# Retention and a gated feed-forward on one core: query order, the x^T blocks kept in DRAM, the work lists and the last products changed together

## The chip, the cores and the metric

The kernel runs on one core of one Trainium2 chip. The metric is the device time of one execution in microseconds (us). A second figure is the span of a profiled execution, from the first to the last instruction of the program that the profiler recorded; it is a little shorter than that execution's own time.

## The reference

For 8 batches and 8 heads, with 576 positions of 64 features, a masked retention is computed, and its result goes through a feed-forward layer:

```
scores = q @ k^T / 8                     # [8, 8, 576, 576]
ret    = scores * gamma_h ** (i - j)     # for i >= j, else 0
x      = (ret @ v), heads side by side   # [4608, 512]
h      = x @ w_in                        # [4608, 2048]
g      = h * erf(softplus(h))
out    = g @ w_out                       # [4608, 512]
```

Everything is float32. The decay lets `ret @ v` be computed in pieces of 128 positions, with a state (a sum of k^T v, 64 x 64 for each head) carried from piece to piece.

## The kernel before

**Attention.** 36 pieces of 128 token rows. Four pieces cover most of a batch (576 = 4 x 128 + 64) and the last 64 rows of two batches share a piece. One piece goes through three stages. `transposes(i)` brings q and k into the layout with features on partitions: for the first 8 pieces by TensorE and an eviction by ScalarE (L317), for the later ones by 32 x 32 transposes on VectorE (L310) of data that was loaded in squares. `scores(i)` computes k^T q by heads (L326) and masks it on VectorE into `sT`. `outputs(i)` multiplies by v (L342), adds the carried state times q (L353), computes the new state k^T v (L367), adds it to the old one in `sums` on VectorE, multiplies it by a decay (L384, GpSimd), asks for the loads of a later piece, scales v of the next piece on GpSimd (`weigh_values`, L298), and evicts to `x`. The list `stages` fixes the order of these stages, and `attend` takes them from it.

**Feed-forward.** Four pieces make a chunk of 512 tokens, `x[g, c]` with c from 0 to 8; the 2048 hidden features are worked in 4 groups g. A block (g, c) has a `First` (x times w_in) and a `Second` (times w_out), each in Strassen form: 7 products in place of 8, of 8 TensorE instructions each (L453, L559). `First` and `Second` of neighbouring blocks alternate, and pieces of attention stand between their products as long as there are any. The very first block uses the plain 8 products (`plain`, L507). Strassen's operands are sums of quarters: of x^T in `operands_x` (VectorE), of the activations in `sums` (VectorE), of the weights in `sums_in` and `sums_out`. `softplus` and `erf` run on ScalarE, each after a table load.

The products of a `Second` add up in PSUM: in tile `a` the products B11, T2, T1, B22 follow each other without clearing, and `take` reads `a` after each of them, into another quarter of `o`. So each of them waits for the take before it. `add` takes in the other products (tiles `e` and `g`).

**Kept in DRAM.** For g = 0 `store_x` writes a chunk of x^T with its Strassen sums to `xd`: 7 blocks of 512 columns (only 4 for c = 0); for g = 1 to 3 `load_x` reads it back. The partial sums of the output go to `od` and come back for the next group.

**Weights.** `load_weights` loads a raw piece, and `rounding` works it into the form used, step by step: two steps on ScalarE, four on VectorE, then a multiplication and an addition on GpSimd (L259, L260), after which the next piece is loaded. `round_weights(n)` takes n steps.

**Order.** Nothing is scheduled by a planner. Each engine executes its instructions in the order in which the program names them. A string of letters written by hand sets the start: `a` is one stage of attention, `p` one plain product, `w` two weight loads, `s` the store of chunk 0, a digit that many rounding steps. All loads and stores but one are issued from SyncE's queue, in program order; a queued transfer whose buffer isn't free holds up those behind it. The table of decays (`cst`) comes in over ScalarE's queue.

Of the kernel before, what the change touches and what calls it, by code (L numbers as in the profile page):

```python
# [11 lines left out]
FP32 = mybir.dt.float32  # L12
# [6 lines left out]
P = 128  # L19
# [3 lines left out]
CONST_COLS = H + NP * P + NP + P + H  # L23
# [7 lines left out]
def decays():  # L31

    gamma = 1.0 - 2.0 ** (-5.0 - np.arange(H, dtype=np.float64))
    pairs = gamma.reshape(2, NP)
    t = np.arange(P)
    gk = pairs.T.reshape(1, H) ** -t[:, None]
    row = pairs.repeat(D, axis=0)
    out = np.where(np.arange(NP) % 2 == 0, row, np.roll(row, D, axis=0))  # L40
    gq = out[:, :, None] ** t[None, None, :] / math.sqrt(D)
    gp = row**P
    tri = t[None, :] >= t[:, None]
    gk2 = gk[t % D]
    return np.concatenate([x.reshape(P, -1) for x in (gk, gq, gp, tri, gk2)], axis=1).astype(np.float32)
# [3 lines left out]
def kernel(  # L49
# [39 lines left out]
    xd = [dram.tile([P, n_dc + 3, TCH], FP32, tag="xd", name="xd") for _ in range(n_ch)]  # L89
# [18 lines left out]
    live = {}  # L108

# [45 lines left out]
    nc.scalar.dma_start(out=cst, in_=consts)  # L155
    ends = [0]
    for m in (H, NP * P, NP, P, H):
        ends.append(ends[-1] + m)
    gk, gq, gp, tri, gk2 = (cst[:, a:b] for a, b in zip(ends, ends[1:]))
    gq = gq.rearrange("p (a i) -> p a i", a=NP)  # L160
    gp = gp.unsqueeze(2).to_broadcast([P, NP, D])
    load(1)
    load(2, "kv")
# [62 lines left out]
    def rounding():  # L226


        while True:
# [29 lines left out]
            nc.gpsimd.tensor_tensor(out=r_f, in0=high_f, in1=r_f, op=ALU.mult)  # L259
            nc.gpsimd.tensor_tensor(out=a_f, in0=a_f, in1=r_f, op=ALU.add)  # L260
            load_weights()
# [12 lines left out]

    tri2 = cpool.tile([P, P], FP32, name="tri2")
    nc.vector.tensor_copy(out=tri2, in_=tri)
    nc.vector.memset(tri2[:D, D:], 0.0)

# [21 lines left out]
    def transposes(i):  # L300
        t = live[i] = loaded.pop(i)
        if i < SQUARES:
            weigh_values(i + 1)
        for name in "qk":
            tT = t[name + "T"] = att.tile([P, NP, P], FP32, tag=name + "T", name=name + "T")
            if i >= SQUARES:
                for _, _, n, r0 in pieces[i]:
                    a = r0 // SQ * D
                    squares = t[name + "s"][:, :, a : a + n // SQ * D].rearrange("p h (a d) -> p h a d", d=D)
                    nc.vector.transpose(  # L310
                        out=tT[:, :, r0 : r0 + n].rearrange("p h (r a) -> p h a r", r=SQ), in_=squares[:, :, :, :SQ]
                    )
            else:
# [3 lines left out]
                nc.scalar.copy(out=tT, in_=pt)  # L317
# [15 lines left out]
    def outputs(i):  # L333
# [5 lines left out]
        o = [ps_at.tile([P, 4, P], FP32, tag="at", name=f"o{j}") for j in range(2)]  # L339
        for p in range(NP):  # L340
            for e in range(2):
                nc.tensor.matmul(  # L342
                    o[p % 2][heads[(e + p) % 2], p // 2, :],
                    lhsT=t["v"][:, 2 * p + e, :],
                    rhs=t["sT"][:, e, p, :],
                    start=(p < 2),
                    stop=(not seen and p >= NP - 2),
                    skip_group_check=True,
                )
        for state, r0, n in seen:  # L350
            for p in range(NP):
                for e in range(2):
                    nc.tensor.matmul(  # L353
                        o[p % 2][heads[(e + p) % 2], p // 2, r0 : r0 + n],
                        lhsT=state[heads[e], p, :],
                        rhs=t["qT"][heads[e], p, r0 : r0 + n],
                        start=False,
                        stop=(p >= NP - 2),
                        skip_group_check=True,
                    )  # L360
        b, s0, n, _ = segments[0]
        if n == P:

            kv = o[0].rearrange("p a i -> p (a i)")[:, 2 * P :].rearrange("p (a d) -> p a d", a=NP)
# [66 lines left out]
    def operands_x(g, c):  # L431
# [8 lines left out]
        if g == 0:  # L440
            store_x(c)
# [302 lines left out]
```

## Time and profile before

| what | value |
|---|---|
| median of 3 runs | 1050.09 us (1050.07 to 1050.46) |
| profiled execution | 1053.23 us, span 1051.5 us |
| TensorE (PE) busy | 1025.0 us, 97% of the span |
| VectorE (DVE) busy | 640.9 us, 61% |
| ScalarE (ACT) busy | 378.3 us, 36% |
| GpSimd (POOL) busy | 132.7 us, 13% |
| moved by DMA | 192.23 MB, 183 GB/s over the span |
| mean granted clock of TensorE | 0.988 |

The time falls into five stretches: the start up to about 75 us, with the first pieces of attention and the plain block; a stretch to about 335 us in which attention stands between the products of the blocks with g = 0; the last three blocks with g = 0; the blocks with g = 1 to 3, which are products alone; and the end, from about 1025 us, where no `First` is left to stand between the products of the last `Second`s. In a timeline line the columns are start, duration, engine, line, operation, output<-inputs, shapes, and the count; in brackets stands how long the engine was idle ahead of it and what ended that.

### The profile page before, as it was taken

The numbers are of one execution on the slowest core, as the hardware profiler recorded it, in microseconds if no ns is written. First come the engines' busy times: TensorE is split into PE (matmuls) and PEld (weight loads), VectorE is DVE, ScalarE is ACT, GpSimd is POOL, SyncE is SP. The second block draws the span as 40 slices with busy tenths as digits, with TensorE's granted clock in tenths as the row PEclk, the third lists the DMA queues.
The fourth block names the chain that finished last, engine by engine and source line by source line (L and its number), as shares of the span: only waits on it lengthen the run. The fifth ranks groups of instructions, "written<-read, shape, count | busy, mean of one in ns | idle before, by whom it ended". The sixth has DMA issues, their size and how long they took to land.

```text
span 1051.5 us, 15730 instructions
## 1 busy us (share of the span) xinstructions
PE 1025.0 (97%) x6322; PEld 879.9 (84%) x6322; DVE 640.9 (61%) x1001; ACT 378.3 (36%) x459; POOL 132.7 (13%) x130
## 2 busy tenths in 40 slices
PE   8889999999899999999999999999999999999997
PEld 7667887778788888888888888888888888888885
DVE  3679888878677654555555655555556544454444
ACT  2243232231332444443434333434443333333341
POOL 2551321221221100100001000110100000000000
PEclk9889999999899999999999999999999999999999
DMA  9989979989995534544455455554343344454432
GB/s 195 254 169 237 242 193 256 217 226 244 219 256 167 188 112 150 190 170 170 159 195 197 155 192 205 189 191 151 150 150 121 150 169 176 165 202 167 171 121 80
DMA packets 146777, 192.23 MB, mean 183 GB/s; under 512 B 96016, under 2 KB 121104, under 8 KB 138640
## 3 DMA queue, kind: packets, MB, share of 16 engines
q1 hardware_dynamic: 146560, 190.88, 60.9%
q8 instruction: 50, 0.82, 0.3%
q10 hardware_dynamic: 144, 0.34, 0.1%
q14 instruction: 23, 0.19, 0.1%
HBM read 137.70 MB, written 53.48 MB: 182 GB/s over the span
## 4 chain that ended last, share of the span: by engine, by line
PE 80%; DMA 9%; DVE 5%; SPq 3%; issue 1%; POOL 0%; ACT 0%; DVEq 0%; POOLq 0%; ACTq 0%
PE a L559 22%; PE a L453 20%; PE g L559 11%; PE g L453 10%; PE e L559 5%; PE e L453 5%; DMA raw_ks<-in_k_dram 3%; SPq L137 2%; PE s L326 2%; DMA od<-o 2%; PE o L342 2%; DMA xd<-x 2%; DVE t L93 1%; DVE o L93 1%; PE o L367 1%
## 5 line engine op out<-in xcount | busy, mean ns | idle before, releaser
L453 PE MATMUL a<-x,wa 128*128 128x256 f32 x1120 | 266.0, 380 | 0.0
L453 PEld LDWEIGHTS a<-x,wa 128*128 128x128 f32 x1120 | 211.6, 190 | 29.4
L559 PE MATMUL a<-wb,s 128*128 128x256 f32 x864 | 205.8, 381 | 2.1 <-DVE o L93 2.1
L559 PEld LDWEIGHTS a<-wb,s 128*128 128x128 f32 x864 | 163.1, 190 | 26.2 <-DVE o L93 2.4
L93 DVE TENSOR_TENSOR o<-a,o 128x512 f32<-128x512 f32 x108 | 74.3, 688 | 107.0 <-PE a L559 104.2
L93 DVE TENSOR_TENSOR t<-g,t 128x512 f32<-128x512 f32 x70 | 48.3, 690 | 148.9 <-ACT t L483 112.5
L453 PE MATMUL g<-x,wa 128*128 128x256 f32 x560 | 133.4, 381 | 0.4 <-DVE o L93 0.3
L453 PEld LDWEIGHTS g<-x,wa 128*128 128x128 f32 x560 | 105.5, 190 | 16.4 <-DVE o L93 1.6
L259 POOL TENSOR_TENSOR wraw<-wraw 128x512 f32<-128x512 f32 x32 | 33.4, 1045 | 462.6 <-DVE wraw L258 242.6
L478 ACT COPY t<-a 128x512 f32<-128x512 f32 x35 | 20.5, 586 | 187.6 <-PE a L453 187.6
L93 DVE TENSOR_TENSOR t<-t,s 128x1024 f32<-128x1024 f32 x72 | 87.2, 1252 | 0.0
L522 ACT ACTIVATE s<-t 128x1024 f32<-128x1024 f32 x72 | 72.1, 1048 | 37.7 <-DVE t L93 37.6
L489 ACT COPY t<-a 128x512 f32<-128x512 f32 x35 | 20.5, 586 | 149.7 <-PE a L453 149.7
L559 PE MATMUL g<-wb,s 128*128 128x256 f32 x288 | 70.3, 388 | 3.8 <-DVE t L93 3.8
L526 ACT ACTIVATE s<-s 128x1024 f32<-128x1024 f32 x72 | 72.1, 1049 | 0.4
L559 PE MATMUL e<-wb,t 128*128 128x256 f32 x288 | 68.6, 381 | 0.0
L559 PE MATMUL a<-wb,t 128*128 128x256 f32 x288 | 68.6, 381 | 0.0
L559 PE MATMUL g<-wb,t 128*128 128x256 f32 x288 | 68.2, 380 | 0.0
L453 PE MATMUL e<-x,wa 128*128 128x256 f32 x280 | 66.7, 381 | 0.0
L559 PEld LDWEIGHTS g<-wb,s 128*128 128x128 f32 x288 | 55.4, 194 | 11.9 <-DVE t L93 4.1
L559 PEld LDWEIGHTS g<-wb,t 128*128 128x128 f32 x288 | 54.6, 190 | 7.5
L559 PEld LDWEIGHTS e<-wb,t 128*128 128x128 f32 x288 | 54.3, 190 | 7.7
(77 smaller groups left out, 1178.5 us busy)
## 6 DMA issues: line engine op xcount, KB each, us to landing
x<-xd SPq DMA_DIRECT2D x24, 1792.0 KB, 10.6
od<-o SPq DMA_DIRECT2D x54, 512.0 KB, 4.1
o<-od SPq DMA_DIRECT2D x27, 1024.0 KB, 7.0
xd<-x SPq DMA_DIRECT2D x8, 1792.0 KB, 7.2
raw_qs<-in_q_dram SPq DMA_DIRECT2D x96, 112.0 KB, 5.0
raw_ks<-in_k_dram SPq DMA_DIRECT2D x96, 112.0 KB, 4.4
raw_k<-in_k_dram SPq DMA_DIRECT2D x64, 128.0 KB, 4.5
raw_v<-in_v_dram SPq DMA_DIRECT2D x64, 128.0 KB, 4.7
```

Source lines behind the costliest of these rows:

```text
L93: nc.vector.tensor_tensor(out=out, in0=in0, in1=in1, op=op)
L137: nc.sync.dma_start(out=t[r0 : r0 + n, e::2, :], in_=heads.rearrange("h p d -> p h d"))
L259: nc.gpsimd.tensor_tensor(out=r_f, in0=high_f, in1=r_f, op=ALU.mult)
L326: nc.tensor.matmul(ps[e][:, p, :], lhsT=t["kT"][heads[e], p, :], rhs=t["qT"][heads[e], p, :], start=True, stop=True)
L342: nc.tensor.matmul(o[p % 2][heads[(e + p) % 2], p // 2, :], lhsT=t["v"][:, 2 * p + e, :], rhs=t["sT"][:, e, p, :], start=(p < 2), stop=(no ...
L367: nc.tensor.matmul(kv[heads[e], p, :], lhsT=t["k"][:, 2 * p + e, :], rhs=t["v"][:, 2 * p + e, :], start=False, stop=(p == NP - 1), skip_gr ...
L453: nc.tensor.matmul(acc[:, j * TH : (j + 1) * TH], lhsT=weights["wa", self.g][:, a, d, j * P : (j + 1) * P], rhs=x[self.g, self.c][a][:, d, :],
L478: nc.scalar.copy(out=self.t1[:, 1], in_=self.a)
L489: nc.scalar.copy(out=self.t2[:, 0], in_=self.a)
L522: nc.scalar.activation(self.s[:, j], t, AF.Softplus)
L526: nc.scalar.activation(self.s[:, j], self.s[:, j], AF.Erf)
L559: nc.tensor.matmul(acc[:, tp, :], lhsT=left[:, j * TH + tp * P : j * TH + (tp + 1) * P], rhs=weights["wb", self.g][:, b, j, :], start=(sta ...
```

## The change

- **Queries in the squares' order.** VectorE's transpose of q writes each 32 x 32 square to consecutive addresses (the order of positions in a piece becomes a, r instead of r, a). The masks and decay tables are permuted on the host to match, ScalarE's eviction permutes q for the first 8 pieces, and the stores of the output put the rows back.
- **Four blocks of x^T in DRAM.** `xd` holds 4 blocks of columns instead of 7. For g of 1 to 3 and c above 0, `operands_x` now recomputes three sums.
- **Evictions by ScalarE.** For g = 0 all four takes of `a` are on ScalarE; two of them were on VectorE.
- **States first.** In `outputs` the new state (products, sum, decay) is computed ahead of the outputs; the loads and the scaling of the next v go to the end of the stage, and `transposes` scales the next v for the first three pieces only.
- **Loads ahead.** A `w` in the string is now one load. The first four weight pieces no longer load the next piece themselves, and six pieces are asked for by letters ahead of the fifth's rounding. Their multiplication and addition go from GpSimd to VectorE. The start string is another one, and `stages` has its two exchanges at other pieces.
- **Table.** `cst` comes in two parts over SyncE's queue and holds a finished mask `tri2`.
- **Last products.** In the last two `Second`s (`rest`) the order is T2, T3, T1, T4, B22 instead of T2, T3, T1, B22, T4, so that tile `a` and the other one alternate. `multiply` and `sums` of the last block stand elsewhere, in two parts. Of the last stores some are issued from ScalarE's queue.

```diff
-    xd = [dram.tile([P, n_dc + 3, TCH], FP32, tag="xd", name="xd") for _ in range(n_ch)]
+    xd = [dram.tile([P, n_dc, TCH], FP32, tag="xd", name="xd") for _ in range(n_ch)]
...
-    nc.scalar.dma_start(out=cst, in_=consts)
+    nc.sync.dma_start(out=cst[:, :CONST_FIRST], in_=consts[:, :CONST_FIRST])
...
-            nc.gpsimd.tensor_tensor(out=r_f, in0=high_f, in1=r_f, op=ALU.mult)
-            nc.gpsimd.tensor_tensor(out=a_f, in0=a_f, in1=r_f, op=ALU.add)
-            load_weights()
+            first = (name, g) == ("wa", 0)
+            engine = nc.vector if first else nc.gpsimd
+            engine.tensor_tensor(out=r_f, in0=high_f, in1=r_f, op=ALU.mult)
+            engine.tensor_tensor(out=a_f, in0=a_f, in1=r_f, op=ALU.add)
+            if not first:
+                load_weights()
...
-        if i < SQUARES:
+        if i < PC - 1:
             weigh_values(i + 1)
...
+                    order = "p h (a r) -> p h a r" if name == "q" else "p h (r a) -> p h a r"
                     nc.vector.transpose(
-                        out=tT[:, :, r0 : r0 + n].rearrange("p h (r a) -> p h a r", r=SQ), in_=squares[:, :, :, :SQ]
+                        out=tT[:, :, r0 : r0 + n].rearrange(order, r=SQ), in_=squares[:, :, :, :SQ]
                     )
...
-        if i in (PC - 1, PC):
+        if i in (PC + 1, 2 * PC - 1):
             stages[-3:-1] = stages[-2], stages[-3]
...
             tt(t1, b12, b11, ALU.subtract)
             tt(t2, b22, t1, ALU.subtract)
             tt(b12, b22, b12, ALU.subtract)
-            tt(t4, b21, t2, ALU.subtract)
+        else:
+            tt(t2, b12, b11, ALU.add)
+            tt(t1, b22, t2, ALU.subtract)
         if g == 0:
             store_x(c)
+        tt(t4, b21, t2, ALU.subtract)
...
-            elif engine == "scalar":
+            else:
                 nc.scalar.copy(out=dst, in_=acc)
-            else:
-                nc.vector.tensor_copy(out=dst, in_=acc)
...
+        def rest(self):
+            e = ps_e.tile([P, 2, OH], FP32, tag="g", name="g2")
+            self.product(T2, self.a, False)
+            self.take(1, 0, self.a)
+            yield
+            self.product(T3, e, True)
+            self.add(1, 1, e)
+            self.store(0, slice(0, OH), nc.scalar)
+            yield
+            self.product(T1, self.a, False)
+            self.take(1, 1, self.a)
+            yield
+            self.product(T4, e, False)
+            self.add(1, 0, e)
+            self.store(1)
+            yield
+            self.product(B22, self.a, False)
+            self.take(0, 1, self.a)
+            for tp, queue in enumerate((nc.sync, nc.scalar)):
+                self.store(0, slice(OH, D_MODEL), queue, (tp,))
+            yield
...
-    for j, what in enumerate("aaaawaaawaa4a1a5asa1a4pa5papapa5p4apa1p4apa5a5a"):
+    for what in "alkakakawkakakawaa3awwa2aasa5caawwapa5p5ppaww4pa5pa5paa5p1":
...
-    attend(after_chunk(1))
+    attend(after_chunk(1) + 1)
     operands_x(0, 1)
-    attend(done[0] + 1)
+    round_weights(4)
```

In the new string `l` is the load of k and v of piece 2, `k` two idle products that keep TensorE occupied, and `c` the second part of the table.

## The prediction

> **What bounds the kernel now.** I read the page's slices first, then busy time by stretch, then PE's waits and the timeline around them.
>
> ```profile
> PE   8889999999899999999999999999999999999997
> ...
> DVE  3679888878677654555555655555556544454444
> ...
> PEclk9889999999899999999999999999999999999999
> DMA  9989979989995534544455455554343344454432
> ```
>
> PE has nearly no idle time after slice 13 (about 340 us); before that VectorE and the DMA engines are as full as PE, and PEclk drops twice in the start and once in slice 11. The stretches, with columns PE, PEld, DVE, ACT and POOL busy, granted clock, DMA share and GB/s:
>
> ```profile
> 25.00:50.00 25.00, 20.16 (x175) 16.52 (x172) 15.61 (x31) 5.75 (x11) 14.13 (x13) 0.80 1.07 250
> 50.00:75.00 25.00, 20.95 (x229) 16.87 (x228) 18.67 (x35) 12.14 (x19) 12.38 (x12) 0.86 0.82 174
> 75.00:300.00 225.00, 218.29 (x2045) 177.20 (x2046) 187.18 (x300) 62.40 (x78) 51.37 (x51) 0.98 1.00 231
> 300.00:1025.00 725.00, 724.85 (x3547) 634.98 (x3546) 400.41 (x606) 287.76 (x339) 49.41 (x45) 1.00 0.47 169
> 1025.00:1051.50 26.50, 18.66 (x83) 15.14 (x81) 12.19 (x17) 3.23 (x3) 0.00 (x0) 0.99 0.24 80
> ```
>
> PE idles 4.8 us, 4.1 us, 6.7 us, 0.2 us and 7.8 us in these. From 300 to 1025 us only fewer products could help, and the change removes none. All gain must come from the first 300 us and the last 26, and the middle can only be spoilt. The busy ends of PE are modelled, so idle of a few tenths is uncertain.
>
> In the start, TensorE waits for a state that GpSimd makes late, since GpSimd stands ahead of it in `weigh_values` for a v that has not landed (the state itself starts at 30.31):
>
> ```profile
> 29.24 1.11 POOL L298 TENSOR_TENSOR raw_v<-raw_v,cst 128x512 f32<-128x512 f32 x1 [7.67 <-DMA raw_v<-in_v_dram]
> ...
> 31.42 1.13 PE L353 MATMUL o<-qT,state 64*64 64x128 f32 x16 [1.63 <-POOL state L384]
> ```
>
> In the stretch with attention, VectorE's transposes wait for q still in flight, and the products that need VectorE wait behind them:
>
> ```profile
> 266.72 1.10 DVE L310 STREAM_TRANSPOSE qT<-raw_qs 128x512 f32<-128x512 f32 x1 [4.91 <-DMA raw_qs<-in_q_dram]
> ...
> 270.16 3.78 PE L559 MATMUL g<-wb,s 128*128 128x256 f32 x8 [2.74 <-DVE t L93]
> ```
>
> From 75 to 300 us VectorE waits 14.0 us for raw_qs and 9.5 us for raw_ks, most of its 37.8 us of idle time there. So transfers, not VectorE's work alone, make it late.
>
> [...] 0.50 from 32 to 40 us, 0.51 from 68 to 75, 0.53 from 269 to 276, each after idle gaps. [...] The transposes that write with a step of four elements (16 bytes) take 1.12 us for 128x512; the half pieces, with a step of two, 0.43 us for 128x256, so 0.85 for as much data[...]. [...] L253 took 1.41 us at 29.48 beside GpSimd and 0.69 without.
>
> **The start (to 80 us).** The cap first: idle 4.8 + 4.1 us, plus half of the PE work done at half clock (about 8.7 us busy from 30 to 41, 4.8 from 68 to 75), 4.3 + 2.4 us: 15.6 us.
> - States first: the new state comes 1.7 us of PE earlier (ahead of L342 and L353), and scaling of the next v moves behind it on GpSimd. The 1.63 us wait goes; what is late next is `sT` on VectorE (2.31 us at 28.11). The state's products (0.6 us) now stand ahead of L342 and cover part.
> - New string: the score mask of piece 7 comes before rounding steps. Before, `sums`, evictions and four rounding operations (65.20 to 69.28) stood ahead of it, and PE waited 3.76 us at 69.93.
> - First four weight pieces: 8 operations of about 0.69 us move to VectorE, +5.5 us; GpSimd loses 8 (1.05 and 1.29 us), and with them some contention. VectorE is busy 41 us by 75 us, mostly after 25 us, so 5.5 us more fits only if it stops waiting: this caps the gain.
> - DMA: one more issue on SyncE's queue ahead of piece 1 (the table, 0.5 us; its 334 KB were moved before too), k and v of piece 2 now behind q of piece 2, and the second half of w_in and w_out later. The last of w_out stands behind some 13 MB (eight pieces of 0.79 MB, 2.1 MB each of w_in and w_out, chunk 0's store, the table, piece 8), which at the 222 GB/s of the first 50 us is there at about 59 us, when its rounding is due; VectorE, stopped there, would hold the evictions of piece 7 behind it for 2 us or so. Within the range.
> - Q's eviction on ScalarE reads with a step; unseen in this trace. Bound: 0 to +0.6 us (its own 0.59 us again) for 8 pieces; two or more PE steps stand between eviction and scores, so I take 0.
>
> Of 15.6 us I take **-7** (range -11 to -2).
>
> **With attention (80 to 335 us).** Cap: idle 6.7 us plus half of 5.8 us at half clock, 9.6 us.
> - `xd` shrinks by 768 KB a store. Six stores here are 4.7 MB of 52.0 MB, 20 us of DMA time at 231 GB/s, just where the share is 1.00. A store takes 7.4 us to land, so the q squares behind it land about 3 us sooner, against the waits of 4.91 and 2.50 us that led to PE's 2.74 and 1.05 us.
> - VectorE loses 10 copies of 0.68 us (6.8 us) and at least 0.27 us on each of 22 transposes of q (6 us; below nothing is excluded, since the writes get denser and reads stay).
> - The copies go to ScalarE, 28% busy here. T1 needs the take after T2; softplus (2.0 us) stands ahead, but T3 and two attention steps lie between. Cost 0.
>
> I take **-7** (-10 to -2).
>
> **Last three blocks with g = 0.** No attention covers here:
>
> ```profile
> 347.41 1.28 ACT L526 ACT_TABLE_LOAD   x1
> 347.92 1.89 PE L559 MATMUL a<-wb,s 128*128 128x256 f32 x8
> ```
>
> Softplus ends at 347.39. The first take (0.59) now comes then, to 348.0, so T1 slips 0.15 us [...]. Erf with its table (1.28 + 2.0 us) stands between the takes: the second ends at 351.9, VectorE's `add` at 352.6 in place of 351.26, and everything behind it is 1.35 us later (x sums, t<-e, `multiply`, add of T4). That add ended at 357.6, needed at 358.28: slack 0.7 us, cost 0.7 to 0.9 us. In the next two blocks slack is 0.4 us, and the recomputed x sums join the last one. Sum about **+3** (0 to +4).
>
> **Blocks with g = 1 to 3.** 24 blocks get 3 VectorE operations (2.61 us for 4, so 1.95 us). In an ordinary block VectorE idles 2.11 us right there (617.51 to 619.62), so they fit, and one rounding step (up to 0.69 us) uses the 0.75 us of slack behind. The trace shows the same spot with more in it, at c = 0: four x sums and a weight sum, 3.2 us:
>
> ```profile
> 599.51 0.68 DVE L93 TENSOR_TENSOR o<-g,o 128x512 f32<-128x512 f32 x1
> ...
> 600.25 1.99 PE L453 MATMUL g<-x,wa 128*128 128x256 f32 x8
> ```
>
> There the product came 0.24 us late (598.28 + 1.73 = 600.01), so about 2.95 us are free, against 2.64 at most. The loads are issued ten products (17 us) ahead and took 10.6 us with 7 blocks of columns. I take **0** (0 to +5); 18.9 MB less of reads hides anyway at a DMA share of 0.47.
>
> **The end.**
>
> ```profile
> 1044.81 4.23 SPq L621 DMA_DIRECT2D out_dram<-o  x8
> ```
>
> From T2 of the block before the last (1022.00) 12 products remain, 12 x 1.727 = 20.7 us, but they take 23.6, with waits of 0.79, 0.55 and 0.78 us, each for a take. Alternating tiles give each take a product of cover (0.69 in 1.73 us); `multiply` (2.35 us) now stands behind the take of T1. PE ends 2.9 us earlier, at about 1042.9. Behind it stood an add and the last stores, to 1049.04, and 2.46 us more; now one take (to 1043.65), one issue on each of two queues (0.45) and the same 2.46: 1046.55 against 1051.5. **-4.9** (-5.5 to -3).
>
> **Sum.** -7 - 7 + 3 + 0 - 4.9 = -15.9 us. The profiled execution took 1053.23 us (span 1051.5 and 1.7 around), 3.1 above the median; against its own time that is 1037.3, against the median of 1050.1 it is **1034**.
>
> **Rivals.**
> - *VectorE holds the start.* Its 5.5 us more, and w_out landing late, leave 3 us; attention gives 3: -3 - 3 + 3 - 4.9 = -8, 1042 us. For it: VectorE 24.8 of 25 us busy from 75 to 100. Against: 23.5 us of its waits are for DMA. Chance 0.26.
> - *All waits go.* -13 - 9 + 1 - 5 = -26, 1024 us. [...] Chance 0.12.
> - *The recomputed x sums hold up the next product,* slower than before. If VectorE is late in each of 24 blocks, say by GpSimd's rounding beside operations with two SBUF inputs, and the S3 product waits 1 us, that is +24 - 16 = +8, 1058 us; it decides from 0.66 us a block. Against: the 0.24 us at c = 0. Chance 0.05.
> - *No effect of the new transpose order* (still 1.1 us): 6 us of VectorE's time stay, and the result is between the first rival and the forecast; counted there.
>
> **How the numbers follow.** The forecast has 0.57; 0.04 of the first rival's 0.26 is its bad end, within 0.2% of before. Adding the worse ends of start and attention gives about 1045; both better ends about 1024; beyond lie the slower case and a clock that drops elsewhere. Range 1023 to 1046. A difference under 0.2% (2 us) is about what a measurement of this kernel can't tell from none. Faster 0.91, same 0.04, slower 0.05.
>
> **What would show it.** Right: PE at L453 `e` of the first Strassen block (77.82) 6 to 9 us earlier; granted clock above 0.9 from 25 to 75; qT transposes at or under 0.85 us; DMA share under 0.95 from 80 to 300; products 1.73 us apart for g above 0; a gap of 0.8 to 1.2 us ahead of S3 in the last three blocks with g = 0; the span's end 4 us or less after the last product. Wrong: gaps ahead of S3 in most blocks with g of 1 to 3, or half clock in three stretches again.

## The result and the profile after

The changed kernel takes 1183.53 us in the median (1181.24 to 1189.19, four runs) against 1050.16 us of the kernel before on the same chip: a ratio of **1.128** (95% interval 1.123 to 1.132), 12.8% slower. The forecast was 1034 us, faster. The profiled execution took 1185.33 us, with a span of 1183.5 us.

Slices of the page after, the same rows as were shown of before:

```profile
PE   8787888888898999999999999999999778877775
...
DVE  3676657656565554666666666667564444443333
...
PEclk9998899998999999999999999999999999888888
DMA  9898858976774232434444245332443222212231
```

Two places have lost time (slices are counted from 0). Up to slice 12 PE is mostly at 7 or 8 where it was mostly at 9, and VectorE and the DMA engines are emptier too: everybody waits for somebody. From slice 31 (about 917 us, the blocks with g = 3) PE is at 7 or 8, at the very end at 5, where it was at 9; the clock falls to 8 from slice 34 on. The middle, between them, is nearly as before.

The three largest waits of PE in the kernel after (columns: us in total, times, longest):

```profile
PE a L571 <- DVE o L99: 49.2, 7, 8.4
PE o L377 <- DVE sums L99: 42.8, 24, 3.5
PE o L377 <- DVE state L373: 13.6, 8, 5.0
```

The kernel before had no wait of PE in its list above 6.2 us. The second and the third line are one wait, 24 + 8 times: the outputs' products (L377) stand behind VectorE, which reads the new state. The timeline around one of them, in the kernel after:

```profile
227.04 0.69 PE L356 MATMUL o<-raw_v,raw_k 128*64 128x64 f32 x16
227.35 0.70 DVE L315 STREAM_TRANSPOSE qT<-raw_qs 128x512 f32<-128x512 f32 x1
227.98 1.04 DVE L315 STREAM_TRANSPOSE kT<-raw_ks 128x512 f32<-128x512 f32 x1
...
229.80 0.41 DVE L99 TENSOR_TENSOR sums<-o,state 128x256 f32<-128x256 f32 x1
...
230.26 1.09 PE L377 MATMUL o<-sT,raw_v 128*64 128x128 f32 x16 [2.54 <-DVE sums L99]
```

The state's products (L356) write the upper half of PSUM tile `o[0]`; `sums` reads it there; the outputs' products write the lower half of the same tile, and start when `sums` has ended. `sums` in turn stands in VectorE's queue behind two transposes, a rounding step and an add. In the kernel before the state's products came last, so no product of that stage stood behind that read.

The first line, 49.2 us, is seven waits in the blocks with g = 3. Around the first of them, in the kernel after:

```profile
924.92 3.19 SPq L654 DMA_DIRECT2D out_dram<-o  x4
928.22 2.46 SPq L565 DMA_DIRECT2D o<-od  x1
...
942.06 0.69 DVE L99 TENSOR_TENSOR o<-a,o 128x512 f32<-128x512 f32 x1 [8.33 <-issue]
...
942.81 1.65 PE L571 MATMUL a<-wb,s 128*128 128x256 f32 x3 [6.04 <-DVE o L99]
...
1166.99 1.89 PE L571 MATMUL a<-wb,s 128*128 128x256 f32 x8
1167.91 4.17 SPq L654 DMA_DIRECT2D out_dram<-o  x4
```

Four stores of the output are issued (3.19 us in all), then the load of the partial sums, whose issue alone takes 2.46 us. From 903.59 to 924.92 SyncE's queue issued nothing: it waited ahead of these stores, 15.8 us of it for VectorE's `o`, and the load stood behind them. The take on VectorE that needs them runs at 942.06 after 8.33 us of idle. The timeline names no releaser here, but the list of VectorE's waits has the load for seven takes of this kind (same columns):

```profile
DVE o L99 <- DMA o<-od: 49.3, 7, 10.7
```

T2's product, which adds to the same tile, waits for the take. The last product starts at 1166.99, and the span ends at 1183.5: 14.6 us after that product, most of it the last stores.

### The profile page after: what moved, and what is told of

Same layout as the page of the kernel before. It is cut to its first block, busy times and chain, and to the rows that moved or that the text cites. A ratio compares the mean times of both kernels' runs of the same rounds, so it can differ in the third digit from the quotient of the medians.

```text
span 1183.5 us, 15806 instructions
## 1 busy us (share of the span) xinstructions
PE 1052.9 (89%) x6322; PEld 894.9 (76%) x6322; DVE 673.0 (57%) x1061; ACT 387.8 (33%) x477; POOL 121.5 (10%) x122
## 4 chain that ended last, share of the span: by engine, by line
PE 62%; DVE 16%; DMA 11%; SPq 4%; issue 3%; ACT 2%; DVEq 0%; ACTq 0%
PE a L571 17%; PE a L464 14%; PE g L464 8%; PE g L571 8%; DMA o<-od 6%; DVE t L99 5%; PE e L571 4%; PE e L464 4%; PE o L377 3%; DVE x L99 3%; DVE o L99 3%; PE s L336 2%; SPq L654 2%; SPq L130 2%; DMA raw_qs<-in_q_dram 2%
## 5 line engine op out<-in xcount | busy, mean ns | idle before, releaser
L571 PE MATMUL a<-wb,s 128*128 128x256 f32 x864 | 218.4, 398 | 49.2 <-DVE o L99 49.2
L571 PEld LDWEIGHTS a<-wb,s 128*128 128x128 f32 x864 | 169.9, 199 | 78.2 <-DVE o L99 52.0
L99 DVE TENSOR_TENSOR o<-a,o 128x512 f32<-128x512 f32 x108 | 74.3, 688 | 183.3 <-PE a L571 111.7
L99 DVE TENSOR_TENSOR t<-g,t 128x512 f32<-128x512 f32 x70 | 48.3, 690 | 137.8 <-ACT t L494 113.0
L377 PE MATMUL o<-sT,raw_v 128*64 128x128 f32 x576 | 44.7, 302 | 56.8 <-DVE sums L99 42.8
L99 DVE TENSOR_TENSOR t<-t,s 128x1024 f32<-128x1024 f32 x72 | 92.4, 1323 | 0.0
L377 PEld LDWEIGHTS o<-sT,raw_v 128*64 128x64 f32 x576 | 34.7, 149 | 62.8 <-DVE sums L99 46.1
L267 POOL TENSOR_TENSOR wraw<-wraw 128x512 f32<-128x512 f32 x28 | 29.2, 1042 | 506.8 <-DVE wraw L264 293.7
L99 DVE TENSOR_TENSOR x<-x 128x512 f32<-128x512 f32 x116 | 75.6, 684 | 1.2
L464 PE MATMUL e<-x,wa 128*128 128x256 f32 x280 | 70.0, 395 | 0.0
L99 DVE TENSOR_TENSOR o<-g,o 128x512 f32<-128x512 f32 x72 | 49.3, 685 | 34.6 <-ACT o L585 27.1
```

Source lines behind the costliest of these rows:

```text
L99: nc.vector.tensor_tensor(out=out, in0=in0, in1=in1, op=op)
L267: engine.tensor_tensor(out=r_f, in0=high_f, in1=r_f, op=ALU.mult)
L377: nc.tensor.matmul(o[p % 2][heads[(e + p) % 2], p // 2, :], lhsT=t["v"][:, 2 * p + e, :], rhs=t["sT"][:, e, p, :], start=(p == 1 or p == 0 ...
L464: nc.tensor.matmul(acc[:, j * TH : (j + 1) * TH], lhsT=weights["wa", self.g][:, a, d, j * P : (j + 1) * P], rhs=x[self.g, self.c][a][:, d, :],
L571: nc.tensor.matmul(acc[:, tp, :], lhsT=left[:, j * TH + tp * P : j * TH + (tp + 1) * P], rhs=weights["wb", self.g][:, b, j, :], start=(sta ...
```

## The experiments

**Theory A**: the shared PSUM tile. **Theory B**: the stores of the output with permuted rows. Rivals were C (the recomputed sums of x^T), D (the start), and others as they arose. All ratios are to the kernel before, measured beside each kernel; 0.001 is 1.05 us. Kernels 2, 3 and 7 leave the output's rows in another order than the reference's. Intervals are 95% ones, and a trace shows one execution of its kernel.

**1. States behind the outputs again (e1_state_last).**

```diff
-        if n == P:
-            kv = flat(o[0])[:, 2 * P :].rearrange("p (a d) -> p a d", a=NP)
...
-                    start=(p == 1 or p == 0 and n < P),
+                    start=(p < 2),
...
+        if n == P:
+            kv = flat(o[0])[:, 2 * P :].rearrange("p (a d) -> p a d", a=NP)
...
+                        start=False,
```

> The changed kernel with one part undone: the state's products, sum and decay stand again behind the outputs' products. Theory A (a shared PSUM tile): with states first, the outputs' products wait 56.4 us in all for VectorE to read the state out of the tile that they write next; undone, these waits go, and with them about half of the 27.9 us that PE was busy longer at half clock: 56 + 14 = 70 us less, about 1113 us, and the wait of these products for VectorE's sums is near zero. Theory B (slow permuted output stores) alone: the shared tile costs nothing that would not be lost otherwise, so the time stays within 10 us of 1183. Rival D (the start string and rounding on VectorE make attention late): VectorE is late anyway, so PE's waits move to the score masks and the time falls by less than 25 us.

1125.43 us, 1.069 (1.068 to 1.071): 0.058 less than the change, 61 us. PE's waits in it:

```profile
PE a L571 <- DVE o L99: 50.0, 7, 9.1
PE s L336 <- DVE kT L315: 6.0, 5, 1.9
```

The waits of the outputs' products (L377 in the kernel after) are gone, those of g = 3 unchanged. A holds, though the gain of 61 us is less than its 70. D does not: under it PE's waits would have moved to the score masks, and no wait for a mask is in the list; the largest new one is 6.0 us of the score products for k's transposes.

**2. Stores in the order of the tile (e2_plain_store).**

```diff
-                        rows = out[b * S + s0 : b * S + s0 + n, os].rearrange("(r a) o -> a r o", r=SQ)
+                        rows = out[b * S + s0 : b * S + s0 + n, os]
```

> The changed kernel, but the stores of the output write the rows in the order in which they lie in the tile (rows within each piece of 128 or 64 are then in the queries' order, not the reference's): same bytes, same 2 KB rows, same number of stores. Theory B: the permuted pattern makes each store slow, the load of od queued behind it lands late, and seven takes wait 49.2 us; undone, these waits go and the half clock behind them (granted clock 0.84 to 0.93 from 900 us on): 49 + 10 = about 59 us less, about 1124 us, with blocks of g = 3 at 24.2 us again. Theory A alone: nothing changes for g = 3, 1183 us within 3. Rival C (the sums of x^T recomputed on VectorE make the blocks of g = 1 to 3 late): no change, since they stay.

1105.41 us, 1.051 (1.048 to 1.053): 0.077 less, 81 us, more than the 59 expected (49 of waits, 10 of clock), because the end, which that sum left out, gains too: from the product in the last but one row of the table below (1061.98 here) to the end of the span it takes 40.6 us in place of 61.7. The stretch that lost PE 12.2 of 100 us in the kernel after is full (columns: PE, PEld, DVE, ACT and POOL busy, clock, DMA share, GB/s):

```profile
900.00:1000.00 100.00, 100.00 (x465) 88.03 (x464) 54.54 (x78) 36.23 (x41) 0.00 (x0) 1.00 0.38 137
```

C is out as the cause of the large loss, since the recomputed sums are still there.

**3. Both (e3_both).** The two edits together.

> Both undone together: states behind the outputs, and output stores in the order of the tile (rows permuted within a piece). If A and B are the whole of the error of the forecast, the time is the forecast's 1034 us, and 1023 to 1054 in any case (1183 - 70 - 59 = 1054 from the traces' waits, if they add up). If a third cause is there (C: recomputed sums; D: start string), it stays above 1060 us, and its waits are the largest that are left.

1047.76 us, 0.995 (0.9935 to 0.9965). The singles were worth 0.058 and 0.077, together 0.135; both at once 0.133. They add up: two separate causes, and the sign of the rest is that of the forecast. Its size is not: the forecast of 1034 us was 0.985 of the kernel before. PE's longest waits in it are small:

```profile
PE s L336 <- DVE kT L315: 7.6, 6, 2.8
PE g L464 <- DVE o L99: 4.0, 6, 0.8
PE p L518 <- DVE wa L268: 2.3, 1, 2.3
```

**4. States first, in a tile of their own (e4_own_tile).**

```diff
-        o = [ps_at.tile([P, NP, P], FP32, tag="at", name=f"o{j}") for j in range(2)]
...
-            kv = flat(o[0])[:, 2 * P :].rearrange("p (a d) -> p a d", a=NP)
+            kv = flat(ps_at.tile([P, NP, P], FP32, tag="at", name="kv"))[:, : 2 * P].rearrange("p (a d) -> p a d", a=NP)
...
+        o = [ps_at.tile([P, NP, P], FP32, tag="at", name=f"o{j}") for j in range(2)]
...
-                    start=(p == 1 or p == 0 and n < P),
+                    start=(p < 2),
```

> States first as in the changed kernel, but the state's products go to a PSUM tile of their own, taken from the same four banks, so that the outputs' products do not wait for VectorE to read it. Permuted stores stay. Theory A: the wait was for the tile, not for the place in the order: the same gain as with the states behind the outputs, about 1113 us; less by some us where five tiles for a piece now share four banks. Rival (the place in the order costs: the state's products and sums hold up the outputs whatever the tile): the time stays near 1183, and PE waits elsewhere for VectorE.

1126.69 us, 1.070 (1.068 to 1.072), the same as states last. So it was the tile and not the place in the order. No gain of the earlier place shows either, but this kernel has a new cost: with five tiles on four banks the score products wait 6.3 us for VectorE's reads of the state, so a gain of that size would be hidden.

**5. Each permuted store cut in four (e5_split_store),** on top of states last.

```diff
-                        queue.dma_start(out=rows, in_=self.o[r0 : r0 + n, half, tp, os])
+                        for a in range(n // SQ):
+                            queue.dma_start(out=rows[a], in_=self.o[r0 + a * SQ : r0 + (a + 1) * SQ, half, tp, os])
```

> States behind the outputs, and each permuted store of the output cut into one store for each a (four of 32 rows, or two for a half piece), so that each has one dimension of 32 rows, four rows apart, of 2 KB. Theory B1 (the store is slow because its outermost dimension counts only 4, whatever the addresses): the waits of the takes for the partial sums go and the time is that with stores in the tile's order, 1048 us, plus 1 to 3 us for three more issues on each queue at the end. Theory B2 (rows four rows apart are slow to write): the time stays near 1125 us. Theory B3 (issues: SyncE needs four times as many, 16 a block at 0.45 us): the load of the partial sums goes out 5 us later than before, which its lead of one block still covers, so no loss.

1073.38 us, 1.019 (1.015 to 1.023): two thirds of the 0.077 are back, with rows as far apart as in the change. B2 is out. What is left are waits for the same takes (14.8 us in seven, in an execution that took 1066.36 us) and an end of 7.3 us behind the last product, where stores in the tile's order leave 4.2. SyncE's queue shows why:

```profile
915.29 8.30 SPq L655 DMA_DIRECT2D out_dram<-o  x16
923.63 0.42 SPq L565 DMA_DIRECT2D o<-od  x1
```

Sixteen issues take 8.3 us, and the load goes out behind them. B3 named these issues but expected no loss from them; they cost.

**6. Permuted stores from ScalarE's queue (e6_act_queue),** on top of states last.

```diff
-                        queue.dma_start(out=rows, in_=self.o[r0 : r0 + n, half, tp, os])
+                        nc.scalar.dma_start(out=rows, in_=self.o[r0 : r0 + n, half, tp, os])
```

> States behind the outputs, and all permuted stores of the output, unchanged in pattern, are issued from ScalarE's queue, so that the load of the partial sums does not stand behind them. Theory B (only the load behind the stores in one queue makes PE wait): the takes no longer wait for it, and the time falls from 1125 to about 1048 us, plus what ScalarE loses by waiting for VectorE's adds ahead of each store (up to 1 us a block, 9 us in all). Theory B4 (the stores fill the DMA engines themselves, whichever queue they come from): the load is as late as before, and the time stays above 1110 us.

1075.74 us, 1.023 (1.020 to 1.026). Neither number: the takes' wait is gone, but PE waits 12.5 us for ScalarE's copies, which now stand behind stores that wait for VectorE, and the end is about as long as in the change (15.0 us behind the last product). It shows that standing in one queue behind the stores was most of it (0.047 of 0.077), and that the other queue isn't free.

**7. Another permutation, with an outer count of 32 (e7_outer32),** on top of states last.

```diff
-                        rows = out[b * S + s0 : b * S + s0 + n, os].rearrange("(r a) o -> a r o", r=SQ)
+                        rows = out[b * S + s0 : b * S + s0 + n, os].rearrange("(a r) o -> r a o", r=SQ)
```

> States behind the outputs, and each output store in one piece with the other permutation: its outermost dimension counts 32 and its inner one 4, rows of 2 KB, neighbours in the pattern 32 rows apart (the rows of a piece come out in another order than the reference's). Theory B1 (outermost count of 4): fast again, 1048 us within 5. Theory B2 (rows that are not consecutive, or a pattern of more than one dimension of rows): slow, 1110 us or more.

1047.95 us, 0.997 (0.995 to 0.998), as fast as plain stores. From its DMA list (KB each, median us from issue to landing):

```profile
out_dram<-o SPq DMA_DIRECT2D x28, 256.0 KB, 2.5
```

The kernel before had 2.4 us for the same store; for the kernel after the list gives no landing times. Rows that are scattered, in two dimensions, are no trouble, and in 5 the distances of the change were none either (1.7 us to landing for a store of 64 KB); an outermost count of 4 is (1.069 in kernel 1, against 0.997 here). **B1 is shown** for these counts: 4 is slow and 32 is not. Why is not shown: the engines of one transfer are not seen in the profile.

**8. One rounding step later (e8_round_later),** on top of split stores. The blocks with g of 1 to 3 lost 4.4 us even with both undone. Around one of the gaps, in that kernel (e3_both), with GpSimd's rounding (L267, and L268 right behind it) beside the multiplication by erf (L99, t<-t,s):

```profile
420.83 1.04 POOL L267 TENSOR_TENSOR wraw<-wraw 128x512 f32<-128x512 f32 x1 [64.96 <-DVE wraw L264]
421.20 3.98 DVE L99 TENSOR_TENSOR t<-t,s 128x1024 f32<-128x1024 f32 x2
...
426.44 1.78 PE L464 MATMUL g<-x,wa 128*128 128x256 f32 x7 [0.83 <-DVE o L99]
```

```diff
-            run(nxt.first(), (1,))
+            run(nxt.first(), () if b.g > 0 else (1,))
             f.multiply()
-            run(b.last(), (0, 1))
+            run(b.last(), (1, 1) if b.g > 0 else (0, 1))
```

> As the kernel with states behind the outputs and split stores, but in the blocks with g above 0 one step of the weights' rounding that stood ahead of the multiplication by erf stands behind it. With both undone, four of the blocks with g of 1 to 3 still lost 1.1 us each: there GpSimd's two operations (started by that step) ran beside VectorE's multiplication, which took 3.98 us for two instead of 2.4. Theory C1 (contention there): the four gaps of 0.8 us ahead of S3 go, 4 us less than the kernel with split stores. Rival (the sums of x^T are too much by themselves): the gaps stay, within 1 us.

1069.18 us, 1.018 (1.014 to 1.022): not told apart from split stores alone, since the runs of either kernel lie over 8 us apart. The wait ahead of S3 went from 4.0 to 0.7 us, so C1's gaps are gone, but with these stores other waits cover it.

**9. Load of the partial sums ahead of the stores (e9_load_ahead),** on top of states last, stores as in the change.

```diff
-            seconds[n - 1].begin()
+            if n == 1:
+                seconds[0].begin()
...
             f.multiply()
+            seconds[n + 1].begin()
             run(b.last(), (0, 1))
```

> States behind the outputs, permuted stores of the output in one piece (outermost dimension of 4) as in the changed kernel, but the load of the partial sums for the next Second is issued ahead of the last two products of the running one, and so ahead of its stores in SyncE's queue. Theory B (the load waits behind slow stores in the same queue): the load lands in time in most blocks, and the time falls from 1125 to about 1050 to 1060 us. Theory B5 (the slow stores keep what comes behind them from moving for more than a block): the stores of one block run into the load of the next, and at least half of the 77 us stays, above 1088 us.

1070.48 us, 1.015 (1.012 to 1.017), above B's 1050 to 1060 and below B5's 1088: 0.055 of the 0.077 are back, and the wait for takes is 0.3 us in place of 50.0. The slow end stays (15.2 us behind the last product). What comes behind the stores instead is the load of x^T, and now PE waits for that:

```profile
PE a L464 <- DMA x<-xd: 6.1, 6, 2.8
```

**10. Split stores, load ahead, rounding step later (e10_split_ahead).** The edits of 5, 8 and 9, on top of states last.

> States behind the outputs, split stores (32 rows each), the load of the partial sums issued ahead of the running block's stores, and one rounding step behind the multiplication by erf. With split stores alone 14.8 us of waits of products for takes were left in the last nine blocks, with the load standing behind 16 issues. Theory B3 (these issues make it late): they go, and with the four gaps of 0.8 us ahead of S3 gone too the time is 1043 to 1050 us. Rival (32 rows still move slower than 128): more than 8 us of waits for takes stay and it is above 1055 us.

1046.54 us, 0.993 (0.991 to 0.995). The issues ahead of the load were what was left, as B3 says for this run: from 380 to 1030 us PE waits for nothing. In the place shown under 8 the multiplication takes 2.35 us again and S3 waits for nothing:

```profile
422.13 2.35 DVE L99 TENSOR_TENSOR t<-t,s 128x1024 f32<-128x1024 f32 x2
...
425.56 1.04 POOL L267 TENSOR_TENSOR wraw<-wraw 128x512 f32<-128x512 f32 x1 [68.70 <-DVE wraw L264]
...
426.43 1.89 PE L464 MATMUL g<-x,wa 128*128 128x256 f32 x8
```

**11. Columns of x put back at the eviction (e11_natural_x),** states last, plain stores, decays in the natural order.

```diff
...
+                dst = x[0, c][:, j:NP:2, at + m : at + m + n].rearrange("p a (r k) -> p a r k", r=SQ)
+                got = o[j][:, :2, m : m + n].rearrange("p a (k r) -> p a r k", r=SQ)
+                tt(dst, got, by, ALU.mult)
```

> States behind the outputs, queries in the squares' order up to the eviction of the outputs to x, which reads PSUM with a step of 32 elements and so puts the columns of x back into the reference's order; the stores of the output are then plain. 72 such evictions of 256 columns took 0.41 us each. Theory E (a read of PSUM with a step costs nothing): as with both parts undone, 1048 us. Rival (it costs like the transposes' write with a step, 0.4 us per 512 elements more): 0.2 us for each of 72, 14 us of VectorE in the stretch with attention, of which the products see a half at most: up to 1055 us.

1048.49 us, 0.995 (0.993 to 0.996). An eviction of 256 columns takes as long with the step as without:

```profile
L99 DVE TENSOR_TENSOR x<-o,cst 128x256 f32<-128x256 f32 x64 | 23.8, 413 | 0.0
```

Theory E holds: 413 ns, as in the kernel before (413).

**12. The rounding step later on that (e12_natural_later).**

> As the kernel with columns put back at the eviction to x, with one rounding step behind the multiplication by erf in the blocks with g above 0. Theory C1 (GpSimd's two operations beside that multiplication cost 1.1 us in each of four blocks): 4 us less than without this move, about 1044 us, and the gaps of 0.8 us ahead of S3 are gone. Rival (another wait takes their place): within 1 us of the kernel without it.

1049.19 us, 0.995 (0.993 to 0.997): the rival was right. The four gaps ahead of S3 are gone, but T2's product now waits three times for the take ahead of it (2.1 us): around 528 us a weight load and a store stand ahead of the load of the partial sums, which goes out 3 us later than in the kernel of 11.

**13. The parts together (f1_best):** the edits of 11, 8 and 9.

> The parts put together: states behind the outputs, columns of x put back at the eviction (so plain stores), the load of the partial sums ahead of the running block's stores, one rounding step behind the multiplication by erf. If what each removed adds up: 1048.5 us of the kernel with columns put back, less 4 us for the four gaps ahead of S3, 1044 us. If the order of the start decides more than these (the kernels alike but for such moves were 1046.5 to 1049.2): 1045 to 1049.

1043.26 us, 0.993 (0.991 to 0.994). From 380 to 1030 us PE waits for nothing. From the third to the fourth row of the table below it takes 459.98 us, exactly as the kernel before; the kernel of 11 takes 464.35. So the 4.4 us of C1 are back here.

**14. Every chunk of x^T stored twice (f2_double_store),** on top of 11.

```diff
         nc.sync.dma_start(out=xd[c], in_=x[0, c][:, :n_dc])
+        nc.sync.dma_start(out=xe[c], in_=x[0, c][:, :n_dc])
```

> States behind the outputs and columns put back at the eviction, and every chunk of x^T is stored twice (the second time to a place that nobody reads): 1 MB more for each of 9 stores, about 6 of them in the stretch with attention. Theory F1 (transfers bound that stretch, so that the time VectorE saved there became waits for k and q): 6 MB at 220 GB/s are 27 us of transfers, and the kernel is 10 to 27 us slower, with more waits of VectorE for raw_qs and raw_ks than their 28 us with both undone. Theory F2 (the order of issue and the buffers bound it, not the bytes): less than 4 us slower, and then the 4.7 MB that the change took out of that stretch gave little for the same reason.

1061.93 us, 1.010 (1.009 to 1.012): 0.015 more than 11, 16 us. VectorE's waits from 75 to 300 us in it:

```profile
DVE qT L316 <- DMA raw_qs<-in_q_dram: 23.3, 9, 5.1
DVE kT L316 <- DMA raw_ks<-in_k_dram: 17.0, 15, 1.9
```

In the kernel of 11 they were 12.1 and 12.2 us. The whole loss is there by the table's second row (330.99 us, kernel 11 has 317.05). F1: bytes count in that stretch.

**15. Four blocks of x^T alone, on the kernel before (f3_four_blocks).** The edits of `xd`, `load_x`, `store_x` and `operands_x` of the change, nothing else.

> The kernel before with one part of the change alone: four blocks of x^T in DRAM, three sums recomputed for g of 1 to 3. By the prediction: about 3 us gained in the stretch with attention (20 us of transfers fewer, against waits of 4.91 and 2.50 us for q), nothing lost later: 1047 us. Theory C1: in blocks where GpSimd rounds beside the multiplication, 1.1 us lost in four or five: +4.4 us, so 1050 to 1052 us, no change. Theory F2 (bytes do not bound the stretch): no gain there, 1053 us or more.

1047.10 us, 0.996 (0.995 to 0.998), as expected, but made up otherwise: 10.0 us gained by the end of the attention in place of 3, and 4.4 lost in the blocks with g of 1 to 3 in place of 0 (table below). F2 is out; C1 has its 4.4 us. From 75 to 300 us only this is left of 23.5 us of waits for q and k:

```profile
DVE kT L310 <- DMA raw_ks<-in_k_dram: 0.2, 1, 0.2
```

**16. The order of the queries alone, on the kernel before (f4_query_order),** with columns put back at the eviction.

> The kernel before with queries in the squares' order alone, columns of x put back at the eviction (stores as before). By the prediction: 22 transposes are 0.41 us shorter in the stretch with attention, 9 us of VectorE's time, worth 3 to 4 us: 1046 us. Theory F1 (transfers bound): VectorE only waits longer for the next squares, and the time stays within 2 us of before.

1052.69 us, 1.000 (0.999 to 1.001). Its waits of VectorE from 75 to 300 us:

```profile
DVE qT L312 <- DMA raw_qs<-in_q_dram: 12.7, 7, 4.8
DVE kT L312 <- DMA raw_ks<-in_k_dram: 12.7, 13, 2.1
```

Before it was 14.0 and 9.5. VectorE is busy 7.3 us less in this stretch, and the time stays as F1 said; but its waits for q and k grew by only 1.9 us, those for TensorE by 5.2. That the shorter transposes merely wait for the next squares is thus shown in small part.

**17 and 18. Loads of k and v earlier in the stage,** on top of 11 (g1_kv_early) and of 13 (g2_best_kv).

```diff
+        load(i + 3, "kv")
+        weigh_values(i + 1)
         c, at = i // PC, i % PC * P
...
-        load(i + 3, "kv")
-        weigh_values(i + 1)
```

> As the kernel with states behind the outputs and columns put back at the eviction (1048.5 us), but the loads of k and v three pieces ahead, and the scaling of the next v, stand again directly behind the state, ahead of the evictions to x. Four blocks alone on the kernel before gained 10.0 us by the end of the attention (last product of S with g = 0 and attention at 313.3 in place of 323.3) and left no wait for q and k; this kernel gained 6 and VectorE still waits 24 us for them. Theory G1 (these loads go out too late in the changed order): the waits for q and k fall by half and the time by about 3 us, 1045. Theory G2 (the bytes and the other order of loads in the first 50 us decide, 250 GB/s from 37.5 to 50 us where the kernel before moved 300): within 1 us of 1048.5.

> The same move on the best kernel so far (1043.3 us: columns put back, partial sums loaded ahead of the stores, one rounding step later). Theory G1: 3 us less, 1040 us. Theory G2: within 1 us of 1043.

1048.83 us, 0.996 (0.995 to 0.998), and 1041.99 us, 0.990 (0.987 to 0.993). The intervals overlap those of 11 and 13: G1 is out for 11, and no gain is shown for 13. The kernel of 18 has the shortest median here, 1.0% faster than the kernel before and 12% faster than the change. Its slices:

```profile
PE   8879999999999999999999999999999999999998
...
PEclk9999999999999999999999999999999999999999
DMA  9989989998984433433354533353333333343422
```

## Why the prediction was wrong, step by step

The prediction gave "slower" a chance of 0.05, for the recomputed sums. The loss came from two parts of the change that none of its rivals names.

Start of the same product in each kernel, in us (B22 of the `Second` named; the last row is the span's end):

| | before | after | both undone | four blocks alone |
|---|---|---|---|---|
| B22, g = 0, c = 0 | 117.55 | 128.34 | 114.32 | 117.57 |
| B22, g = 0, c = 5 | 323.25 | 374.84 | 316.34 | 313.27 |
| B22, g = 0, c = 8 | 401.44 | 456.27 | 396.09 | 391.46 |
| B22, g = 3, c = 0 | 861.42 | 921.06 | 860.43 | 855.78 |
| B22, g = 3, c = 6 | 1006.46 | 1121.77 | 1005.76 | 1000.83 |
| end of span | 1051.5 | 1183.5 | 1046.4 | 1045.8 |

One profile a kernel is little for differences of a few us in the start: eight kernels (1, 3 and 5 to 10) have the same instructions in the same order up to the table's second row, and stand between 111.49 and 119.94 us at the first row, and between 312.86 and 320.39 at the second. "Both undone" lies in the middle of them.

- **"States first" was costed as an earlier state with cover** (the 1.63 us wait goes, 0.6 us of products cover part). The step that failed: it moved the state's products ahead of L342 without asking what they leave in PSUM, and who must read it before the same tile is written again. The wait it added, with its queue (transposes, rounding steps, adds ahead of `sums` on VectorE), cost 61 us. It was no unknown of size but a wait that the prediction did not list. With a tile of its own for the state's products it is gone (kernel 4, 1.070 in place of 1.128). Whether the tile or the bank makes the wait, no run here tells.
- **The permuted output stores had no term at all.** Same bytes, and but for the last blocks the same 2 KB rows and the same number of stores; the outermost count fell from 128 to 4 (from 64 to 2 for half pieces). That cost 81 us: in the takes' waits, in the clock behind them (0.86 from 1025 us; 0.50 from 943 to 947 us, where T2's product lasts 3.78 us in place of 1.89), and at the end, where the span ends 14.6 us after the last product is done and not within the 4 us forecast. The prediction read of a store only its bytes and its issue, and the term "2.46" us at the end was carried over from a store of another shape. In kernel 2, without these waits, the clock is 1.00 from 900 to 1000 us; that idle time lowers it was the author's assumption.
- **The rest of the sum**, read from the kernel with both undone, came to -5.1 us of span in place of -15.9:
  - Start and attention: -6.9 at g = 0, c = 5 in place of -14. The first Strassen `e` comes 5.8 us earlier (72.00; 70.72 to 76.53 in the others with this start), of which 3.2 are left at the table's first row; the gains of start and attention did not add. Bytes count in that stretch (14), and VectorE waits 27.9 us for q and k there, in the kernel before 23.5 and with four blocks alone 0.2; that coming earlier is what makes it wait longer is argued, not shown. Four blocks alone gave the whole cap of 9.6, 10.0 us (forecast: -7 with the transposes), and the transposes alone nothing in the time (16). The term "VectorE loses 6 + 6.8 us" was priced as if it could be cashed beside transfers that were late anyway; of its two parts only the transposes were tried alone. Why the changed start keeps 3 us less than four blocks alone stays open; from 25 to 50 us it moved 215 GB/s and the kernel before 250, and the place of the loads of k and v does not decide it for kernel 11 (17).
  - Last three blocks with g = 0: +1.6 for +3, inside its range.
  - Blocks with g of 1 to 3: +4.4 for 0 (and 0.3 more up to the next row), near the end of its range. The mechanism was the one of the third rival (GpSimd's rounding beside operations with two SBUF inputs), but in four blocks out of 24, where the two coincide, and 1.1 us each. The proof by the block with c = 0 used a stretch (592 to 600 us) with no GpSimd operation in it. The two multiplications took 3.98 us beside GpSimd, 2.35 without.
  - End: -4.4 for -4.9, right in mechanism and nearly in size. In the kernel with both undone the last product starts at 1040.30, is done at 1042.19, and the span ends 4.2 us later.
- **What the prediction asked the profile to show.** The kernel before had a granted clock of 0.50 from 32 to 40 us, 0.51 from 68 to 75 and 0.53 from 269 to 276. In the kernel after the granted clock from 25 to 75 us is 0.93, q's transposes take 0.70 us, and the DMA share from 75 to 300 us is 0.81: all three as forecast, in a kernel that is 12.8% slower. The last was met for a wrong reason, since PE was late: with both undone the share is 0.97. The marks that spoke were the first Strassen `e`, at 79.90 us in place of 6 to 9 us ahead of 77.82, and the end of the span.

## What to carry to other kernels

Before an operation is moved ahead, list what it writes in PSUM and who must read it before the next product may write that tile: a product that was last of its stage had nobody behind it, and its move cost 61 us here. Before a store's pattern is changed, count its outermost dimension: here 4 in place of 128 cost 81 us with equal bytes and equal rows, and what stood behind it in its queue was late too (49.2 us of PE's waits). In a stretch where transfers are late, ask for bytes first: here 4.7 MB less gave 10 us, and transposes that took 10 us less in all gave nothing.

## What the hardware showed that was not expected

- A store of 256 KB in 2 KB rows landed in 2.5 us with its rows in order (outermost count of 128) and with neighbours 32 rows apart (count of 32). With a count of 4 the load behind it took 2.46 us to issue in place of about 0.4, and VectorE got its data at 942.06, 11 us after the end of that issue; cut into four, each store of 32 rows landed in 1.7 us and the load behind took 0.42 us to issue, but 16 issues took 8.3 us.
- VectorE's read of PSUM with a step of 32 elements (128 bytes) cost nothing: 413 ns for 256 columns with or without. The step of four elements in its transposes' write did: 0.70 us for 512 elements without it, 1.10 with it. A step of two cost nothing: in the kernel after, 256 elements took 0.40 us with it (k) and 0.42 without (q).
